# Block 0 of a Mish MLP by single x tiles, with one accumulation group per PSUM bank

## The chip, the cores and the metric

The kernel runs on one core of one Trainium2 chip. The metric is the device time of one execution in microseconds; lower is better. TensorE (PE in the profile, with PEld for its weight loads) multiplies; VectorE (DVE) and ScalarE (ACT) read the results out of PSUM; GpSimd (POOL) only prepares constants; SyncE (SP) and ACT issue the DMAs.

## The reference

```python
B, S, D, F = 1, 2048, 512, 1792        # bf16 inputs x, w1, b1, w2
def reference(x, w1, b1, w2):
    h = jnp.einsum("bsd,df->bsf", x, w1) + b1
    sp = jnp.log1p(jnp.exp(-jnp.abs(h))) + jnp.where(h > 0, h, jnp.zeros_like(h))
    act = h * jnp.tanh(sp)             # Mish
    return jnp.einsum("bsf,fd->bsd", act, w2)
```

Two matrix products with a Mish between them: x (2048 x 512) by w1 (512 x 1792) plus the bias, Mish, and then by w2 (1792 x 512).

## The kernel before

The 2048 rows of x are taken in four blocks of 512 (`NSB`, `SBW`). For each block the first product (mm1) makes h transposed, one f tile of 128 at a time: 14 f tiles (`FT`), each an accumulation over four k tiles (`KT`) of D, with w1 as the weights and x transposed (`xT`) as the moving operand of 512 columns. ScalarE applies Mish with the bias straight from PSUM into `a_sb` (L164). The second product (mm2) then makes four output tiles of 128 rows, each an accumulation over the 14 f tiles (L195); VectorE copies them to `o_sb` (L199) and SP stores them (L177). The order on every engine is the order in which the program is written: all mm1 of a block, its four mm2, the next block. There is no scheduler; each engine follows its own instruction list and waits on semaphores, which the small class `Stream` sets (`wait`, `mark`).

PSUM has eight banks in use. mm1 uses banks 4 to 7 in turn (`bank1`, L158), so an f tile has to wait for the Mish of the f tile four before it (L168). mm2 uses banks 0 to 3 in turn.

Blocks 1 to 3 get `xT` by transposing DMAs (L100). Block 0 is loaded as it is and transposed by PE: `half_T(h)` (L119) takes half h of the block, 256 rows, waits for its load, and for each k makes two transposes into one bank of 0 to 3; VectorE (even k, L132) and ScalarE (odd k, L135) copy them into `xT`. `first_mm1(h, ks)` (L137) multiplies the columns of one half, 256 of them, by the weights of f tiles 0 to 3 (`F0`) for the listed k tiles, into banks 4 to 7. Each half opens its own accumulation (`start=(k == 0)`), the second only once the first is complete.

The queues at the front: SP issues the two halves of x (256 KB each, a partition getting two neighbouring rows, so 2 KB in one piece, L86-87), then w1 of f tiles 4-7, w1 of f tiles 8-13, w2, and the three transposing loads. ACT issues w1 of f tiles 0-3 in two loads, k tiles 0-1 and 2-3 (L89-90), and the bias. PE starts with six dummy matmuls of 512 columns (L148), then `half_T(0)`, two dummies of 256 columns (`FILL`, L152), and the order of L204 to L215:

```python
        first_mm1(0, (0, 1))
        half_T(1)
        first_mm1(0, (2, 3))
        ...
        first_mm1(1, range(KT))
        for t in range(F0, FT):
            mm1(t)
```

Of the kernel before, what the change touches and what calls it, by code (L numbers as in the profile page):

```python
# [4 lines left out]

P = 128
N_WARM = 6
FILL = (256, 256)


class Stream:
# [20 lines left out]
def bass_standalone__dense_activation_mish__prompt_kernel(  # L32
# [8 lines left out]
    ACT = mybir.ActivationFunctionType  # L41
    ALU = mybir.AluOpType
    BF, F32 = dt.bfloat16, dt.float32

    _, S, D = x.shape
    F = w1.shape[1]
    KT, FT, SBW, C = D // P, F // P, 512, D - P
    NSB, JT = S // SBW, SBW // P
    assert (S, D, F) == (2048, 512, 1792)
    x2, out2 = x[0], out[0]  # L50
    w1v = w1.rearrange("(k p) f -> p k f", p=P)
    w2v = w2.rearrange("(j p) d -> p j d", p=P)
    F0 = 4

    with ExitStack() as es:
        def sb(name, shape, t):
            return es.enter_context(nc.sbuf_tensor(name, shape, t))

        x_nat = sb("x_nat", [P, JT, D], BF)
        xT = sb("xT", [P, KT, S], BF)  # L60
        w1_sb = sb("w1_sb", [P, KT, F], BF)
        w2_sb = sb("w2_sb", [P, FT, D], BF)
        b1_nat = sb("b1_nat", [FT, P], BF)
        b1_sb = sb("b1_sb", [P, FT], F32)
        ones = sb("ones", [P, P], BF)
        ident = sb("ident", [P, P], BF)
        a_sb = sb("a_sb", [P, NSB * FT, SBW], BF)
        o_sb = sb("o_sb", [P, NSB * JT, D], BF)
        ps = es.enter_context(nc.psum_tensor("ps", [P, 8, 512], F32))

        def sem(name):
            return es.enter_context(nc.semaphore(name))

        sp = Stream(nc.sync, None)
        pe = Stream(nc.tensor, sem("c_pe"))
        dve = Stream(nc.vector, sem("c_dve"))
        act = Stream(nc.scalar, sem("c_act"))
        pool = Stream(nc.gpsimd, sem("c_pool"))

        def load(q, dst, src, name, transpose=False):  # L80
            s = sem(name)
            (q.eng.dma_start_transpose if transpose else q.eng.dma_start)(dst, src).then_inc(s, 16)
            return (s, 16)


        x0v = x2[0:SBW, :].rearrange("(h p j) d -> p h j d", h=2, j=2)  # L86
        t_xn = [load(sp, x_nat[:, 2 * h:2 * h + 2, :], x0v[:, h], "s_xn%d" % h) for h in range(2)]
        t_w1k = []
        for k in (0, 2):  # L89
            t_w1k += [load(act, w1_sb[:, k:k + 2, 0:F0 * P], w1v[:, k:k + 2, 0:F0 * P], "s_w1k%d" % k)] * 2  # L90
        t_b1 = load(act, b1_nat[:, :], b1.rearrange("(j p) -> j p", p=P), "s_b1")
        t_w1 = {}
        for a, b in ((4, 8), (8, FT)):
            t = load(sp, w1_sb[:, :, a * P:b * P], w1v[:, :, a * P:b * P], "s_w1_%d" % a)
            for f in range(a, b):
                t_w1[f] = t
        t_w2 = load(sp, w2_sb[:, :, :], w2v, "s_w2")
        t_xT = [None]
        for s in range(1, NSB):
            t_xT.append(load(sp, xT[:, :, s * SBW:(s + 1) * SBW], x2[s * SBW:(s + 1) * SBW, :], "s_xT%d" % s, True))  # L100


        t_ones = pool.mark(pool.eng.memset(ones[:, :], 1.0))  # L103
        pool.wait(t_ones)
        t_id = pool.mark(pool.eng.affine_select(ident[:, :], ones[:, :], pattern=[[1, P]], compare_op=ALU.is_equal,  # L105
                                                fill=0.0, base=0, channel_multiplier=-1))
        act.eng.preload_act_table(ACT.Mish)  # L107


        c_w = nc.const_aps.tensor(1.0, [P, P], BF)  # L110
        c_m = nc.const_aps.tensor(1.0, [P, 512], BF)

        def dummy(n=512):
            nc.tensor.matmul(ps[:, 7, 0:n], c_w, c_m[:, 0:n], start=True, stop=True)  # L114

        HB = SBW // 2
        t_cp = [[None] * KT for _ in range(2)]

        def half_T(h):  # L119

            pe.wait(t_xn[h])
            for k in range(KT):
                if h == 1:
                    pe.wait(t_cp[0][k])
                psb = ps[:, k, 0:HB // 2].bitcast(BF)
                for j in range(2):
                    mm = nc.tensor.transpose(psb[:, j * P:(j + 1) * P], x_nat[:, 2 * h + j, k * P:(k + 1) * P], ident[:, :])  # L127
                t = pe.mark(mm)
                dst = xT[:, k, h * HB:(h + 1) * HB]
                if k % 2 == 0:  # L130
                    dve.wait(t)
                    t_cp[h][k] = dve.mark(nc.vector.tensor_copy(dst, psb))  # L132
                else:
                    act.wait(t)
                    t_cp[h][k] = act.mark(act.eng.activation(dst, psb, ACT.Copy))  # L135

        def first_mm1(h, ks):  # L137

            cs = slice(h * HB, (h + 1) * HB)
            for k in ks:  # L140
                for f in range(F0):
                    pe.wait(t_w1k[k], t_cp[h][k])
                    mm = nc.tensor.matmul(ps[:, 4 + f, cs], w1_sb[:, k, f * P:(f + 1) * P], xT[:, k, cs],  # L143
                                          start=(k == 0), stop=(k == KT - 1))
                    if h == 1 and k == KT - 1:
                        mish(f, pe.mark(mm))

        for _ in range(N_WARM):  # L148
            dummy()
        pe.wait(t_id)  # L150
        half_T(0)
        for n in FILL:  # L152
            dummy(n)


        t_mish = {}

        def bank1(t):  # L158
            return 4 + t % 4

        def mish(t, t_mm):
            act.wait(t_b1c, t_mm)
            f = t % FT
            t_mish[t] = act.mark(act.eng.activation(a_sb[:, t, :], ps[:, bank1(t), :], ACT.Mish, bias=b1_sb[:, f:f + 1]))  # L164

        def mm1(t):
            s, f = divmod(t, FT)
            pe.wait(t_mish.get(t - 4), t_w1.get(f), t_xT[s])  # L168
            for k in range(KT):
                mm = nc.tensor.matmul(ps[:, bank1(t), :], w1_sb[:, k, f * P:(f + 1) * P],  # L170
                                      xT[:, k, s * SBW:(s + 1) * SBW], start=(k == 0), stop=(k == KT - 1))
            mish(t, pe.mark(mm))

        def store(q, i, lo, hi, tok):
            q.wait(tok)
            rows = out2[i * P:(i + 1) * P, :] if i >= JT else o0v[:, i // 2, i % 2, :]
            q.eng.dma_start(rows[:, lo:hi], o_sb[:, i, lo:hi]).then_inc(s_out, 16)  # L177

        s_out = sem("s_out")
        o0v = out2[0:SBW, :].rearrange("(h p j) d -> p h j d", h=2, j=2)  # L180
        n_out = 0
        t_ev = {}

        def mm2(i):
            nonlocal n_out
            s, j = divmod(i, JT)
            pe.wait(t_w2)
            last = i == NSB * JT - 1
            parts = [(0, C, i % 4), (C, D, (i + 1) % 4)] if last else [(0, D, i % 4)]
            for lo, hi, bank in parts:  # L190
                pe.wait(*([t_ev[bank]] if bank in t_ev else [t_b1c, t_cp[1][1], t_cp[1][3]]))
                for f in range(FT):
                    t = s * FT + f
                    pe.wait(t_mish[t])
                    mm = nc.tensor.matmul(ps[:, bank, 0:hi - lo], a_sb[:, t, j * P:(j + 1) * P], w2_sb[:, f, lo:hi],  # L195
                                          start=(f == 0), stop=(f == FT - 1))
                t_mm = pe.mark(mm)
                dve.wait(t_mm)
                t_ev[bank] = dve.mark(nc.vector.tensor_copy(o_sb[:, i, lo:hi], ps[:, bank, 0:hi - lo]))  # L199
                store(sp, i, lo, hi, t_ev[bank])  # L200
                n_out += 1


        first_mm1(0, (0, 1))  # L204
        half_T(1)
        first_mm1(0, (2, 3))
        pe.wait(t_b1)
        psb1 = ps[:, 0, 256:256 + FT // 2].bitcast(BF)
        pe.wait(t_cp[1][0])
        t_b1t = pe.mark(nc.tensor.transpose(psb1, b1_nat[:, :], ident[0:FT, 0:FT]))  # L210
        dve.wait(t_b1t)
        t_b1c = dve.mark(nc.vector.tensor_copy(b1_sb[:, :], psb1))  # L212
        first_mm1(1, range(KT))
        for t in range(F0, FT):
            mm1(t)  # L215
        for s in range(NSB):
            for j in range(JT):
                mm2(s * JT + j)
            if s + 1 < NSB:
                for f in range(FT):  # L220
                    mm1((s + 1) * FT + f)
        sp.eng.wait_ge(s_out, 16 * n_out)


# [26 lines left out]
```

## Time and profile before

| | |
|---|---|
| median of 3 runs | 106.61 us (105.97 to 107.19) |
| the profiled execution | 107.43 us, of which the span from the first to the last instruction is 106.2 us |
| PE busy | 102.3 us, 96% of the span |
| ACT, DVE busy | 40.6 us (38%), 12.5 us (12%) |
| moved by DMA | 7.94 MB in 12417 packets |

How to read the rows: a row of the timeline has the start and the time of a run of like instructions, the engine (SPq and ACTq are the DMA-issuing queues), the line of the kernel, what is written and read, and in brackets how long the engine had been idle and what ended that. A row of the chain has the start, the time, and the work that the end of the program hung on then. A row of the windows has for each stretch its length, the busy time of each engine with its instructions, TensorE's granted clock, the mean busy share of the DMA engines, and GB/s. The clock column reads 1.00 throughout, also where matmuls follow each other at half rate, so the rate has to be read from the matmuls' starts. Matmul durations overlap: the time of one is its start to its modelled end.

### The profile page before, as it was taken

The numbers are of one execution on the slowest core, as the hardware profiler recorded it, in microseconds if no ns is written. First come the engines' busy times: TensorE is split into PE (matmuls) and PEld (weight loads), VectorE is DVE, ScalarE is ACT, GpSimd is POOL, SyncE is SP. The second block draws the span as 40 slices with busy tenths as digits, with TensorE's granted clock in tenths as the row PEclk, the third lists the DMA queues.
The fourth block names the chain that finished last, engine by engine and source line by source line (L and its number), as shares of the span: only waits on it lengthen the run. The fifth ranks groups of instructions, "written<-read, shape, count | busy, mean of one in ns | idle before, by whom it ended". The sixth has DMA issues, their size and how long they took to land.

```text
span 106.2 us, 1146 instructions
## 1 busy us (share of the span) xinstructions
PE 102.3 (96%) x503; PEld 48.7 (46%) x503; DVE 12.5 (12%) x22; ACT 40.6 (38%) x61; POOL 0.7 (1%) x6
## 2 busy tenths in 40 slices
PE   6798999999999999999999999999999999999992
PEld 2486444444444444444444444444444444444462
DVE  0210000022112000021122000021122000011223
ACT  0631988500005888600005777700004888700000
POOL 2000000000000000000000000000000000000000
DMA  2999999911111000001111000001111000001111
GB/s 60 330 374 357 348 286 244 141 40 49 49 49 49 0 0 6 0 0 49 49 49 49 0 0 3 0 6 49 49 49 49 0 0 0 0 0 54 51 49 49
DMA packets 12417, 7.94 MB, mean 75 GB/s; under 512 B 6780, under 2 KB 12156, under 8 KB 12412
## 3 DMA queue, kind: packets, MB, share of 16 engines
q1 hardware_dynamic: 11840, 7.34, 25.1%
q10 hardware_dynamic: 572, 0.53, 1.6%
q8 instruction: 4, 0.07, 0.3%
q14 instruction: 1, 0.01, 0.0%
HBM read 4.20 MB, written 2.10 MB: 59 GB/s over the span
## 4 chain that ended last, share of the span: by engine, by line
PE 94%; DMA 3%; ACT 1%; DVE 0%; issue 0%
PE ps L195 46%; PE ps L170 42%; PE ps L143 4%; DMA x_nat<-in_x_dram 3%; PE ps L127 1%; ACT a_sb L164 1%; PE ps L114 0%; DVE o_sb L199 0%; PE ps L210 0%
## 5 line engine op out<-in xcount | busy, mean ns | idle before, releaser
L164 ACT ACTIVATE a_sb<-ps,b_sb 128x512 bf16<-128x512 f32 x56 | 37.9, 688 | 47.0 <-PE ps L170 44.9
L195 PE MATMUL ps<-w_sb,a_sb 128*128 128x512 bf16 (+2 forms) x238 | 49.0, 366 | 0.0
L170 PE MATMUL ps<-xT,w_sb 128*128 128x512 bf16 x208 | 45.6, 379 | 0.5 <-ACT a_sb L164 0.5
L195 PEld LDWEIGHTS ps<-w_sb,a_sb 128*128 128x128 bf16 x238 | 22.8, 98 | 25.9
L170 PEld LDWEIGHTS ps<-xT,w_sb 128*128 128x128 bf16 x208 | 20.3, 98 | 25.1 <-ACT a_sb L164 0.8
L199 DVE CAST o_sb<-ps 128x512 bf16<-128x512 f32 (+2 forms) x17 | 11.2, 660 | 84.7 <-PE ps L195 84.7
L143 PE MATMUL ps<-xT,w_sb 128*128 128x256 bf16 x32 | 4.6, 297 | 0.0
L114 PE MATMUL ps<-const-bfloat16-1.0 128*128 128x512 bf16 (+1 forms) x8 | 3.3, 572 | 0.8 <-PEq L236 0.8
L143 PEld LDWEIGHTS ps<-xT,w_sb 128*128 128x128 bf16 x32 | 3.4, 109 | 0.7
L135 ACT ACTIVATE xT<-ps 128x256 bf16<-128x256 bf16 x4 | 1.4, 382 | 2.7 <-PE ps L127 2.7
L107 ACT ACT_TABLE_LOAD x1 | 1.3, 1283 | 2.5 <-issue 2.5
L127 PE MATMUL ps<-ident,x_nat 128*128 128x128 bf16 x16 | 1.6, 262 | 0.6 <-DMA x_nat<-in_x_dram 0.6
L127 PEld LDWEIGHTS ps<-ident,x_nat 128*128 128x128 bf16 x16 | 1.3, 117 | 1.5 <-issue 1.5
L132 DVE COPY xT<-ps 128x256 bf16<-128x256 bf16 x4 | 1.1, 292 | 6.6 <-PE ps L127 6.5
L114 PEld LDWEIGHTS ps<-const-bfloat16-1.0 128*128 128x128 bf16 x8 | 1.0, 137 | 1.9 <-issue 1.9
L105 POOL TENSOR_SCALAR_AFFINE_SELECT ident<-ones 128x128 bf16<-128x128 bf16 x1 | 0.3, 294 | 0.1
L212 DVE CAST b_sb<-ps 128x14 f32<-128x14 bf16 x1 | 0.2, 173 | 0.8 <-PE ps L210 0.8
L103 POOL MEMSET ones<- 128x128 bf16 x1 | 0.2, 205 | 0.3 <-POOLq L236 0.3
L210 PEld LDWEIGHTS ps<-ident,b_nat 14*128 14x128 bf16 x1 | 0.1, 90 | 0.2 <-issue 0.2
L210 PE MATMUL ps<-ident,b_nat 14*128 14x14 bf16 x1 | 0.2, 177 | 0.0
L236 POOL MEMSET const-bfloat16-1.0<- 128x1 bf16 x1 | 0.1, 103 | 0.0
L236 POOL MEMSET const-uint8-127<- 128x1 uint8 x1 | 0.1, 103 | 0.0
(2 smaller groups left out, 0.2 us busy)
## 6 DMA issues: line engine op xcount, KB each, us to landing
out_dram<-o_sb SPq DMA_DIRECT2D x15, 128.0 KB, 1.7
w_sb<-in_w_dram SPq DMA_DIRECT2D x1, 1792.0 KB, 12.2
w_sb<-in_w_dram SPq DMA_DIRECT2D x1, 768.0 KB, 7.6
w_sb<-in_w_dram ACTq DMA_DIRECT2D x2, 256.0 KB, 4.4
x_nat<-in_x_dram SPq DMA_DIRECT2D x2, 256.0 KB, 3.7
w_sb<-in_w_dram SPq DMA_DIRECT2D x1, 512.0 KB, 5.9
out_dram<-o_sb SPq DMA_DIRECT2D x1, 96.0 KB, 1.6
xT<-in_x_dram SPq DMA_TRANSPOSE x3, 5.7
```

What stands on the lines that cost most here:

```text
L105: t_id = pool.mark(pool.eng.affine_select(ident[:, :], ones[:, :], pattern=[[1, P]], compare_op=ALU.is_equal, fill=0.0, base=0, channel_mu ...
L107: act.eng.preload_act_table(ACT.Mish)
L114: nc.tensor.matmul(ps[:, 7, 0:n], c_w, c_m[:, 0:n], start=True, stop=True)
L127: mm = nc.tensor.transpose(psb[:, j * P:(j + 1) * P], x_nat[:, 2 * h + j, k * P:(k + 1) * P], ident[:, :])
L132: t_cp[h][k] = dve.mark(nc.vector.tensor_copy(dst, psb))
L135: t_cp[h][k] = act.mark(act.eng.activation(dst, psb, ACT.Copy))
L143: mm = nc.tensor.matmul(ps[:, 4 + f, cs], w1_sb[:, k, f * P:(f + 1) * P], xT[:, k, cs], start=(k == 0), stop=(k == KT - 1))
L164: t_mish[t] = act.mark(act.eng.activation(a_sb[:, t, :], ps[:, bank1(t), :], ACT.Mish, bias=b1_sb[:, f:f + 1]))
L170: mm = nc.tensor.matmul(ps[:, bank1(t), :], w1_sb[:, k, f * P:(f + 1) * P], xT[:, k, s * SBW:(s + 1) * SBW], start=(k == 0), stop=(k == KT ...
L195: mm = nc.tensor.matmul(ps[:, bank, 0:hi - lo], a_sb[:, t, j * P:(j + 1) * P], w2_sb[:, f, lo:hi], start=(f == 0), stop=(f == FT - 1))
L199: t_ev[bank] = dve.mark(nc.vector.tensor_copy(o_sb[:, i, lo:hi], ps[:, bank, 0:hi - lo]))
L210: t_b1t = pe.mark(nc.tensor.transpose(psb1, b1_nat[:, :], ident[0:FT, 0:FT]))
```

## The change

Block 0's x is loaded as tile 0, tile 1 (128 rows, 128 KB each) and tiles 2-3 (256 KB), a partition getting one row of 1 KB per tile. Each tile is transposed by itself: two k tiles into one bank, copied by VectorE (k 0-1) and ScalarE (k 2-3) into two column blocks of `xT`. Tiles 0 and 1 use banks 0 to 3, and tiles 2 and 3 the same again.

The matmuls of f tiles 0 to 3 run in the order in which tiles and weights come: tile 0 with k 0-1 (128 columns), tile 1 with k 0-1 (128 columns), tiles 0-1 with k 2 (256 columns), then the transposes of tiles 2 and 3, tiles 0-1 with k 3, tiles 2-3 with k 0-1, the bias, tiles 2-3 with k 2-3. Only the very first matmul into a bank carries the accumulation start. The two dummies of 256 columns are gone; the six of 512 stay. f tiles 4 to 7 of block 0 go into banks 0 to 3, which the transposes have used, and the others into banks 4 to 7 as before. The bias is copied into a zeroed 128 x 128 tile and transposed as 128 rows. `a_sb` is indexed by f tile and row instead of by block and f tile. The w1 and w2 loads keep their sizes; from f tile 4 on and for the blocks 1 to 3 the order of the matmuls is the same.

```diff
-        x0v = x2[0:SBW, :].rearrange("(h p j) d -> p h j d", h=2, j=2)
-        t_xn = [load(sp, x_nat[:, 2 * h:2 * h + 2, :], x0v[:, h], "s_xn%d" % h) for h in range(2)]
+        for j in range(2):
+            t_xn[j] = load(sp, x_nat[:, j, :], x2[j * P:(j + 1) * P, :], "s_xn%d" % j)
+        t_xn[2] = t_xn[3] = load(sp, x_nat[:, 2:4, :], x2[2 * P:4 * P, :].rearrange("(j p) d -> p j d", p=P), "s_xn2")
...
+        t_bz = dve.mark(nc.vector.memset(b1_pad[:, :], 0.0))
...
+        def transpose_x(j):
+            pe.wait(t_xn[j], t_id)
+            for h, eng in ((0, dve), (1, act)):
+                bank = 2 * (j % 2) + h
+                pe.wait(*free[bank])
+                psb = ps[:, bank, 0:P].bitcast(BF)
+                for i in range(2):
+                    k = 2 * h + i
+                    mm = nc.tensor.transpose(psb[:, i * P:(i + 1) * P], x_nat[:, j, k * P:(k + 1) * P], ident[:, :])
+                eng.wait(pe.mark(mm))
+                dst = xT[:, 2 * h:2 * h + 2, j * P:(j + 1) * P]
+                src = psb.rearrange("p (k t) -> p k t", k=2)
+                t = eng.mark(nc.vector.tensor_copy(dst, src) if eng is dve else act.eng.activation(dst, src, ACT.Copy))
+                t_cp[j, h] = t
+                free[bank] = [t]
...
+        def mm1_step(s, f, k, bank, js=None):
+            n = BLOCKS[s]
+            lo, hi = (0, n) if js is None else (js[0] * P, (js[-1] + 1) * P)
+            first = k == 0 and lo == 0
+            if first:
+                pe.wait(*free[bank])
+            pe.wait(t_w1[k, f])
+            if s:
+                pe.wait(t_xT[s])
+            else:
+                pe.wait(*[t_cp[j, k // 2] for j in (js or range(N0))])
+            return nc.tensor.matmul(ps[:, bank, lo:hi], w1_sb[:, k, f * P:(f + 1) * P],
+                                    xT[:, k, starts[s] + lo:starts[s] + hi], start=first, stop=(k == KT - 1 and hi == n))
...
+        for n in WARM:
+            dummy(n)
+        transpose_x(0)
+        transpose_x(1)
+        def first(js, ks):
             for k in ks:
                 for f in range(F0):
+                    mm = mm1_step(0, f, k, 4 + f, js)
+                    if k == KT - 1 and js[-1] == N0 - 1:
+                        mish(0, f, 4 + f, pe.mark(mm))
+        first((0,), (0, 1))
+        first((1,), (0, 1))
+        first((0, 1), (2,))
+        transpose_x(2)
+        transpose_x(3)
+        dve.wait(t_b1, t_bz)
+        t_b1p = dve.mark(nc.vector.tensor_copy(b1_pad[0:FT, :], b1_nat[:, :]))
+        first((0, 1), (3,))
+        first((2, 3), (0, 1))
+        pe.wait(t_b1p, *free[0])
+        psb1 = ps[:, 0, 0:P // 2].bitcast(BF)
+        t_b1t = pe.mark(nc.tensor.transpose(psb1, b1_pad[:, :], ident[:, :]))
         dve.wait(t_b1t)
+        t_b1c = dve.mark(nc.vector.tensor_copy(b1_sb[:, :], psb1[:, 0:FT]))
+        free[0] = [t_b1c]
+        first((2, 3), (2, 3))
+        for f in range(F0, FT):
+            mm1(0, f, {4: 0, 5: 1, 6: 2, 7: 3}.get(f, 4 + f % 4))
+        for i in range(N0):
+            mm2(i, 0, D, i)
```

More of the change, by code (lines that the diff above doesn't have):

```diff
@@ L6 @@
 P = 128
-N_WARM = 6
-FILL = (256, 256)
+WARM = (512,) * 6
+BLOCKS = (512, 512, 512, 512)
 class Stream:
@@ L46, in bass_standalone__dense_activation_mish__prompt_kernel @@
     F = w1.shape[1]
-    KT, FT, SBW, C = D // P, F // P, 512, D - P
-    NSB, JT = S // SBW, SBW // P
-    assert (S, D, F) == (2048, 512, 1792)
+    KT, FT = D // P, F // P
+    assert (S, D, F) == (2048, 512, 1792) and sum(BLOCKS) == S
     x2, out2 = x[0], out[0]
@@ L52, in bass_standalone__dense_activation_mish__prompt_kernel @@
     w2v = w2.rearrange("(j p) d -> p j d", p=P)
+    starts = [sum(BLOCKS[:i]) for i in range(len(BLOCKS) + 1)]
     F0 = 4
+    N0 = BLOCKS[0] // P
     with ExitStack() as es:
@@ L57, in sb @@
             return es.enter_context(nc.sbuf_tensor(name, shape, t))
-        x_nat = sb("x_nat", [P, JT, D], BF)
+        x_nat = sb("x_nat", [P, N0, D], BF)
         xT = sb("xT", [P, KT, S], BF)
@@ L63, in bass_standalone__dense_activation_mish__prompt_kernel @@
         b1_nat = sb("b1_nat", [FT, P], BF)
+        b1_pad = sb("b1_pad", [P, P], BF)
         b1_sb = sb("b1_sb", [P, FT], F32)
@@ L66, in bass_standalone__dense_activation_mish__prompt_kernel @@
         ident = sb("ident", [P, P], BF)
-        a_sb = sb("a_sb", [P, NSB * FT, SBW], BF)
-        o_sb = sb("o_sb", [P, NSB * JT, D], BF)
+        a_sb = sb("a_sb", [P, FT, S], BF)
+        o_sb = sb("o_sb", [P, S // P, D], BF)
         ps = es.enter_context(nc.psum_tensor("ps", [P, 8, 512], F32))
@@ L83, in load, with load_w1 @@
             return (s, 16)
-        x0v = x2[0:SBW, :].rearrange("(h p j) d -> p h j d", h=2, j=2)
-        t_xn = [load(sp, x_nat[:, 2 * h:2 * h + 2, :], x0v[:, h], "s_xn%d" % h) for h in range(2)]
-        t_w1k = []
-        for k in (0, 2):
-            t_w1k += [load(act, w1_sb[:, k:k + 2, 0:F0 * P], w1v[:, k:k + 2, 0:F0 * P], "s_w1k%d" % k)] * 2
+        def load_w1(q, ks, a, b):
+            return load(q, w1_sb[:, ks, a * P:b * P], w1v[:, ks, a * P:b * P], "s_w1_%d_%d" % (ks.start, a))
+        t_xn, t_w1, t_w2 = [None] * N0, {}, {}
+        for ks in (slice(0, 2), slice(2, 4)):
+            t = load_w1(act, ks, 0, F0)
+            for f in range(F0):
+                for k in range(ks.start, ks.stop):
+                    t_w1[k, f] = t
+        for j in range(2):
+            t_xn[j] = load(sp, x_nat[:, j, :], x2[j * P:(j + 1) * P, :], "s_xn%d" % j)
+        t_xn[2] = t_xn[3] = load(sp, x_nat[:, 2:4, :], x2[2 * P:4 * P, :].rearrange("(j p) d -> p j d", p=P), "s_xn2")
         t_b1 = load(act, b1_nat[:, :], b1.rearrange("(j p) -> j p", p=P), "s_b1")
-        t_w1 = {}
         for a, b in ((4, 8), (8, FT)):
-            t = load(sp, w1_sb[:, :, a * P:b * P], w1v[:, :, a * P:b * P], "s_w1_%d" % a)
+            t = load_w1(sp, slice(0, KT), a, b)
             for f in range(a, b):
-                t_w1[f] = t
-        t_w2 = load(sp, w2_sb[:, :, :], w2v, "s_w2")
+                for k in range(KT):
+                    t_w1[k, f] = t
+        t = load(sp, w2_sb[:, :, :], w2v, "s_w2")
+        for f in range(FT):
+            t_w2[f] = t
         t_xT = [None]
-        for s in range(1, NSB):
-            t_xT.append(load(sp, xT[:, :, s * SBW:(s + 1) * SBW], x2[s * SBW:(s + 1) * SBW, :], "s_xT%d" % s, True))
+        for s in range(1, len(BLOCKS)):
+            lo, hi = starts[s], starts[s + 1]
+            t_xT.append(load(sp, xT[:, :, lo:hi], x2[lo:hi, :], "s_xT%d" % s, True))
+        t_bz = dve.mark(nc.vector.memset(b1_pad[:, :], 0.0))
         t_ones = pool.mark(pool.eng.memset(ones[:, :], 1.0))
@@ L111, in bass_standalone__dense_activation_mish__prompt_kernel, with dummy @@
         c_m = nc.const_aps.tensor(1.0, [P, 512], BF)
-        def dummy(n=512):
+        def dummy(n):
             nc.tensor.matmul(ps[:, 7, 0:n], c_w, c_m[:, 0:n], start=True, stop=True)
[L116 to L121, printed above, removed]
-            for k in range(KT):
[L123 to L135, printed above, removed]
@@ L137, in first_mm1 @@
-        def first_mm1(h, ks):
-            cs = slice(h * HB, (h + 1) * HB)
+        free = [[] for _ in range(8)]
+        t_cp = {}
+        t_mish = {}
+        def transpose_x(j):
[13 more added lines that the diff above has]
+                free[bank] = [t]
@@ new lines, in mish @@
+        def mish(s, f, bank, t_mm):
+            n = BLOCKS[s]
+            act.wait(t_b1c, t_mm)
+            t = act.mark(act.eng.activation(a_sb[:, f, starts[s]:starts[s + 1]], ps[:, bank, 0:n], ACT.Mish,
+                                            bias=b1_sb[:, f:f + 1]))
+            t_mish[s, f] = t
+            free[bank] = [t]
+        def mm1_step(s, f, k, bank, js=None):
+            n = BLOCKS[s]
+            lo, hi = (0, n) if js is None else (js[0] * P, (js[-1] + 1) * P)
[9 more added lines that the diff above has]
+                                    xT[:, k, starts[s] + lo:starts[s] + hi], start=first, stop=(k == KT - 1 and hi == n))
@@ new lines, in mm1, with mm2_step @@
+        def mm1(s, f, bank):
+            for k in range(KT):
+                mm = mm1_step(s, f, k, bank)
+            mish(s, f, bank, pe.mark(mm))
+        s_out = sem("s_out")
+        n_out = 0
+        def mm2_step(i, f, lo, hi, bank):
+            s = max(b for b in range(len(BLOCKS)) if starts[b] <= i * P)
+            if f == 0:
+                pe.wait(*free[bank])
+            pe.wait(t_w2[f], t_mish[s, f])
+            return nc.tensor.matmul(ps[:, bank, 0:hi - lo], a_sb[:, f, i * P:(i + 1) * P], w2_sb[:, f, lo:hi],
+                                    start=(f == 0), stop=(f == FT - 1))
@@ new lines, in put, with mm2 @@
+        def put(i, lo, hi, bank, t_mm):
+            nonlocal n_out
+            dve.wait(t_mm)
+            t = dve.mark(nc.vector.tensor_copy(o_sb[:, i, lo:hi], ps[:, bank, 0:hi - lo]))
+            free[bank] = [t]
+            sp.wait(t)
+            sp.eng.dma_start(out2[i * P:(i + 1) * P, lo:hi], o_sb[:, i, lo:hi]).then_inc(s_out, 16)
+            n_out += 1
+        def mm2(i, lo, hi, bank):
+            for f in range(FT):
+                mm = mm2_step(i, f, lo, hi, bank)
+            put(i, lo, hi, bank, pe.mark(mm))
@@ L140, in first_mm1 @@
+        for n in WARM:
[3 more added lines that the diff above has]
+        def first(js, ks):
             for k in ks:
                 for f in range(F0):
[L142 to L201, printed above, removed]
@@ L204, in bass_standalone__dense_activation_mish__prompt_kernel @@
[L204 to L210, printed above, removed]
-        dve.wait(t_b1t)
[L212 to L221, printed above, removed]
+                    mm = mm1_step(0, f, k, 4 + f, js)
@@ new lines, in bass_standalone__dense_activation_mish__prompt_kernel @@
+        t_b1t = pe.mark(nc.tensor.transpose(psb1, b1_pad[:, :], ident[:, :]))
+        dve.wait(t_b1t)
+        t_b1c = dve.mark(nc.vector.tensor_copy(b1_sb[:, :], psb1[:, 0:FT]))
[5 more added lines that the diff above has]
+            mm2(i, 0, D, i)
+        for s in range(1, len(BLOCKS)):
+            for f in range(FT):
+                mm1(s, f, 4 + f % 4)
+            for i in range(starts[s] // P, starts[s + 1] // P):
+                if i < S // P - 1:
+                    mm2(i, 0, D, i % 4)
+                else:
+                    mm2(i, 0, D - P, i % 4)
+                    mm2(i, D - P, D, (i + 1) % 4)
```

## The prediction

> **What bounds the kernel now.** I read the page first, for the busy shares, then the chain of work that ended last, for where TensorE (PE) is not streaming.
>
> ```profile
> span 106.2 us, 1146 instructions
> PE 102.3 (96%) x503; PEld 48.7 (46%) x503; DVE 12.5 (12%) x22; ACT 40.6 (38%) x61; POOL 0.7 (1%) x6
> ...
> 0.81 3.25 DMA x_nat<-in_x_dram
> ...
> 4.20 1.01 PE ps L127 x8
> 5.21 0.43 PE ps L114 x2
> 5.63 1.41 PE ps L143 x8
> 7.04 0.45 PE ps L127 x8
> 7.49 0.87 PE ps L143 x8
> 8.36 0.11 PE ps L210
> 8.47 1.65 PE ps L143 x14
> 10.12 0.68 ACT a_sb L164
> ...
> 10.84 8.81 PE ps L170 x40
> 19.65 12.09 PE ps L195 x56
> ...
> 92.17 12.13 PE ps L195 x70
> ...
> 104.33 0.29 DVE o_sb L199
> ```
>
> From 10.84 us to 104.3 us the chain is PE alone: 56 matmuls of 512 columns take 12.09 us, 0.216 us each, without a gap. The change leaves the order and number of these matmuls alone (40, then 56 seven times in turn), so what it can move is the instant at which f tile 4 begins, 10.84 us here. I call it E. What follows E lasts 106.2 - 10.84 = 95.4 us.
>
> Before E the timeline shows PE's rate and the two places where it stands still.
>
> ```profile
> 0.84 2.72 PE L114 MATMUL ps<-const-bfloat16-1.0 128*128 128x512 bf16 x6 [0.84 <-PEq L236]
> ...
> 4.20 1.01 PE L127 MATMUL ps<-ident,x_nat 128*128 128x128 bf16 x8 [0.64 <-DMA x_nat<-in_x_dram]
> ...
> 5.43 1.61 PE L143 MATMUL ps<-xT,w_sb 128*128 128x256 bf16 x8
> ...
> 6.88 0.61 PE L127 MATMUL ps<-ident,x_nat 128*128 128x128 bf16 x8
> 7.19 0.51 DVE L132 COPY xT<-ps 128x256 bf16<-128x256 bf16 x2 [1.87 <-PE ps L127]
> ...
> 8.40 1.92 PE L143 MATMUL ps<-xT,w_sb 128*128 128x256 bf16 x16
> ...
> 10.10 4.23 ACT L164 ACTIVATE a_sb<-ps,b_sb 128x512 bf16<-128x512 f32 x7 [2.14 <-PE ps L143]
> ...
> 10.84 8.81 PE L170 MATMUL ps<-xT,w_sb 128*128 128x512 bf16 x40 [0.52 <-ACT a_sb L164]
> ```
>
> PE waits 0.64 us for the first half of x and 0.52 us for the first Mish, which frees bank 4. And it has two rates. The six dummies of 512 columns take 2.72 us, 0.45 each against 0.216 later: about half speed. Eight matmuls of 256 columns run from 5.43 to 6.88, 1.45 us, where eight at full rate take 0.87 (7.49). With 0.213 us slow and 0.108 fast, 5.6 of the eight were slow, so the rate doubled near 5.43 + 5.6 x 0.213 = 6.6 us. I use 0.107 slow and 0.056 fast for 128 columns (0.45 us for eight transposes at 7.04).
>
> The transfers in front of all this:
>
> ```profile
> 0.80 0.98 ACTq L82 DMA_DIRECT2D w_sb<-in_w_dram  x2
> 0.81 0.87 SPq L82 DMA_DIRECT2D x_nat<-in_x_dram  x2
> ...
> w_sb<-in_w_dram ACTq DMA_DIRECT2D x1, 256.0 KB, 3.9
> ...
> x_nat<-in_x_dram SPq DMA_DIRECT2D x1, 256.0 KB, 4.2
> w_sb<-in_w_dram ACTq DMA_DIRECT2D x1, 256.0 KB, 4.9
> ...
> 1.00:2.53 1.53, 1.53 (x5) 0.47 (x4) 0.00 (x0) 0.00 (x0) 0.30 (x2) 1.00 0.45 84
> 2.53:3.03 0.50, 0.50 (x3) 0.12 (x1) 0.00 (x0) 0.48 (x1) 0.00 (x0) 1.00 0.87 270
> 3.03:3.56 0.53, 0.53 (x2) 0.00 (x0) 0.00 (x0) 0.53 (x1) 0.00 (x0) 1.00 0.93 226
> 3.56:3.96 0.40, 0.00 (x0) 0.00 (x0) 0.00 (x0) 0.27 (x1) 0.00 (x0) 1.00 0.96 328
> 3.96:4.66 0.70, 0.47 (x5) 0.49 (x6) 0.06 (x1) 0.00 (x0) 0.00 (x0) 1.00 1.06 386
> 4.66:5.35 0.69, 0.69 (x8) 0.62 (x6) 0.53 (x2) 0.49 (x2) 0.00 (x0) 1.00 1.07 380
> ```
>
> The first four rows are issues; the number after the KB is the time to landing. Each queue issues a load every 0.43 to 0.49 us, so the second x half starts at 1.25 us and the second w1 load at 1.29. The landings are: x half 0 at 4.06 (the chain), w1 for k 0-1 at 0.80 + 3.9 = 4.7, x half 1 at 5.45, w1 for k 2-3 at 6.2. The last column of the windows is GB/s; times the window's length it gives 129, 264, 384, 515, 785 and 1047 kB moved by the ends of the six rows. One load is 262 kB. If they are served one behind the other in order of issue, x half 0 is through at 3.03, w1 k 0-1 at 3.96, x half 1 at 4.66 and w1 k 2-3 at 5.35; each landed 1.03, 0.74, 0.79 and 0.85 us later. The same lag each time is what supports this order.
>
> **The change part by part.**
>
> *Arrivals.* x comes as 131, 131 and 262 kB on SP, alternating with the two w1 loads on ACT. By the running totals: x tile 0 through at 2.53, landed 3.3 to 3.6; w1 k 0-1 (393 kB) through just past 3.56, landed 4.3 to 4.6; x tile 1 (524 kB) in the place that w1 k 0-1 has now, landed 4.7; w1 k 2-3 (785 kB) 5.5; x tiles 2-3 6.2. For tile 1, which decides, the bounds are 3.8 (262 kB through at 3.03 and the smallest lag, if no w1 went ahead of it) and 5.45 (where x half 1 lands now). I take 4.7, the row with the same total. That a tile now comes in pieces of half the size (1 KB rows) has its row in the w1 loads, whose rows are 1 KB too.
>
> *Head of PE.* The dummies end at 3.56 as now. T0 (four transposes) starts at 3.56 and ends at 3.99; PE then waits 0.7 us for tile 1. T1: 4.7 to 5.13. Tile 0's eight matmuls (k 0-1, four f tiles, 128 columns): 8 x 0.107, to 5.98. Tile 1's eight: slow until 6.6 (5.8 of them), 2.2 fast, to 6.72. The two fillers (0.43 us in the chain) are gone; they covered the copies, and here that cover is T1 and the other tile's matmuls: VectorE's copy of two columns blocks, 0.26 us by its row and begun 0.31 us after its transposes, is done at about 5.4 for tile 1 where PE wants it at 5.98.
>
> *The rest of block 0 from 6.72, all at full rate:* k 2 of tiles 0-1, 4 x 0.108 = 0.43; eight transposes 0.45 (tiles 2-3 landed at 6.2, wanted at 7.15); k 3, 0.43; k 0-1 of tiles 2-3, 0.87; the bias transpose 0.11, as now though with 128 rows; k 2-3 of tiles 2-3, 0.87. Together 3.16, which puts E at 9.88. The copies of tiles 2-3 lie beside k 3: the second VectorE copy ends 0.31 + 2 x 0.26 = 0.83 us after the transposes start, PE wants it after 0.88. If that cover failed by a copy, it would cost 0.26.
>
> *f tiles 4 to 7 in banks 0 to 3.* Today the last sixteen matmuls start at 8.40 and would be over at 8.40 + 16 x 0.108 = 10.13; f tile 4 starts at 10.84, behind the first Mish. So the wait is worth 0.71 (0.52 by the idle column alone, which models matmul ends late). It goes. Next late would be bank 4 for f tile 8: it starts at E + 16 x 0.216 = 13.3, and the first Mish ends near 10.2. Banks 0 to 3 were emptied by the copies before the last sixteen matmuls.
>
> *Edits at nothing.* One accumulation start per bank instead of two, the new shape of a_sb, the padded bias (a small VectorE copy and a memset, both long before PE's bias transpose at 8.9; today PE takes the bias at 8.36 without a wait). SP issues one load more, so everything behind it on SP starts 0.43 later:
>
> ```profile
> w_sb<-in_w_dram SPq DMA_DIRECT2D x1, 1792.0 KB, 12.2
> w_sb<-in_w_dram SPq DMA_DIRECT2D x1, 768.0 KB, 7.6
> ...
> w_sb<-in_w_dram SPq DMA_DIRECT2D x1, 512.0 KB, 5.9
> ...
> 3.38 16.74 SPq L82 DMA_TRANSPOSE xT<-in_x_dram  x3
> ```
>
> Issued from 1.73 us on, the 512 KB of f tiles 4-7 land at 7.6, then 8.1 (wanted at 9.9); the 768 KB by 10.3 (wanted at 13.3); w2 by 15.4 (wanted at E + 40 x 0.216 = 18.5). The transposing loads leave SP at 20.1, then 20.5; the first store follows its matmuls by then.
>
> *Sum.* E goes from 10.84 to 9.88, so 0.96 us less: span 105.2, and the profiled execution's 107.43 would be 106.5. That execution is 0.8 us above the median of the three runs, and slow PE at the front is one thing in which it may differ from them. If PE ran fast from the first transpose, today's head would be 4.20 + 0.45 + 0.22 + 0.87 + 0.45 = 6.2, as w1 k 2-3 lands, then 0.87 + 0.11 + 2.44 (8.40 to 10.84) = 9.6; the new one 4.7 + 0.22 + 0.87 = 5.8, plus 3.16 = 8.95. That is 0.67. Between the two I take 0.9: 106.61 - 0.9 = **105.7 us**, 0.85% less. About 1% is what a measurement of this kernel can tell from no change, so the forecast is a gain that lies within that.
>
> **The rivals.**
>
> *The clock is late (slower).* PE worked slowly for 2.72 us before its gap of 0.64 and 2.4 after it, 5.1 in all, ahead of the doubling at 6.6. The new head has no fillers and a gap of 0.7 at 4.0 to 4.7. If a gap there starts the count anew and 5.1 us of unbroken work are needed, the doubling comes at 4.7 + 5.1 = 9.8: tile 1's matmuls end at 6.84, 2.98 us of slow work do 1.49 of the 3.16, and E is 9.8 + 1.67 = 11.5. That is 0.65 later than now: 107.3. It is slower than before once the doubling comes after 8.5 us (6.84 + 3.16 + half of what lies between 6.84 and it exceeds 10.84). For it: the slow first 2.72 us alone did not bring full rate. Against: the present gap of 0.64, almost as long, did not prevent it at 6.6, and if only the 2.4 us behind the gap count, the doubling comes at 7.1 and the gain is still 0.7. [...]
>
> *The queues share evenly.* If SP's and ACT's loads took turns packet by packet, w1 k 2-3 would end together with x tiles 2-3, at 1047 kB, and land at 6.2. Slow PE reaches it at 6.72 and loses nothing; fast PE would wait from 5.8 to 6.2: gain about 0.3 to 0.6, 106.1. Against it: x half 1, in 2 KB pieces, and w1 k 0-1, in 1 KB pieces, would now both land at 5.4; w1 k 0-1 landed at 4.7. [...]
>
> *Tile 1 lands late, and only the Mish wait goes.* At 5.45, T1 ends at 5.88, and tile 0's and tile 1's matmuls at 7.1; E is 10.25, a gain of 0.6: 106.0. For it: three small loads on SP, each with a lag of its own. That tile 0 be no earlier than half 0 is now (4.06) would by itself change nothing, as T0 would still end before tile 1 comes.
>
> *Tile 1 lands early.* At 3.8 to 4.2 the matmuls of tile 0 start by w1 k 0-1's 4.3 to 4.6, and E is about 9.6, a gain of 1.2: 105.4.
>
> **How the numbers follow.** Forecast 0.50 (105.7; 105.4 to 106.0), early tile 1 0.13 (105.4), late tile 1 0.15 (106.0), even sharing 0.05 (106.1), late clock 0.17 (107.3). The range runs from 104.9, the early case with the runs' scatter (0.6 below their median), to 107.3, the clock case. Faster by over 1% is below 105.54: most of the early case and a third of the forecast, 0.28. Slower by over 1% is above 107.7: the clock case reaches from 106.6 to 108.9 (slow through all of the head, E = 6.84 + 2 x 3.16 = 13.2), and I put 0.10 of its 0.17 above that line. The rest is 0.62.
>
> **What the profile would show.** Right: transposes from about 3.6 us, a wait of PE for x near 4.0 to 4.7, full rate from 6.6, no wait of the f tile 4 group for Mish, E near 9.9, and 95.4 us behind it. Wrong: a landing of x tile 1 away from 4.7 moves E by up to its own size; 256-column matmuls still 0.21 us apart after 7 us is the clock; a wait of PE for w1 at k 2 is the sharing; and a gap anywhere after E would be something I have not seen.

## The result

| | kernel before | changed kernel |
|---|---|---|
| median of 20 runs | 106.81 us (105.97 to 107.35) | 105.94 us (105.34 to 106.74) |
| profiled execution | 107.43 us, span 106.2 us | 105.42 us, span 104.2 us |

The ratio is 0.9922, 95% interval 0.9896 to 0.9948: 0.83 us less (0.56 to 1.11). In a later series it was 0.9927 (0.9899 to 0.9954). Executions about 2 us longer, which came in all three series of experiments and in whose four profiles PE's rate doubles only at 8.7 to 10.2 us, are left out of the ratios.

The two profiled executions lie 2.0 us apart, more than twice what the ratio gives. The chain of the changed kernel, start and time in us, then what:

```profile
span 104.2 us, 1154 instructions
PE 100.7 (97%) x500; PEld 48.1 (46%) x509; DVE 12.7 (12%) x24; ACT 40.3 (39%) x61; POOL 0.7 (1%) x6
...
1.27 2.93 DMA x_nat<-in_x_dram
...
4.25 0.51 PE ps L142 x4
4.76 1.33 PE ps L170 x20
6.09 0.02 issue
6.11 0.62 PE ps L142 x8
6.73 1.40 PE ps L170 x12
8.12 0.06 PE ps L226
8.18 0.87 PE ps L170 x8
...
9.11 8.58 PE ps L170 x39
17.69 2.16 PE ps L186 x10
...
102.36 0.29 DVE o_sb L192
```

No ACT stands ahead of f tile 4 any more. (The 39 and 10 stand for 40 and 56 with breaks: a few matmul records are missing from this trace.) Starts are read better from the timeline:

```profile
0.84 2.72 PE L126 MATMUL ps<-const-bfloat16-1.0 128*128 128x512 bf16 x6 [0.84 <-PEq L259]
...
3.35 0.63 PE L142 MATMUL ps<-ident,x_nat 128*128 128x128 bf16 x4
...
4.25 0.51 PE L142 MATMUL ps<-ident,x_nat 128*128 128x128 bf16 x4 [0.27 <-DMA x_nat<-in_x_dram]
...
4.59 1.49 PE L170 MATMUL ps<-xT,w_sb 128*128 128x128 bf16 x20
...
6.11 0.62 PE L142 MATMUL ps<-ident,x_nat 128*128 128x128 bf16 x8
...
6.56 1.56 PE L170 MATMUL ps<-xT,w_sb 128*128 128x256 bf16 x12
...
8.02 9.67 PE L170 MATMUL ps<-xT,w_sb 128*128 128x256 bf16 x47
...
8.83 6.13 ACT L153 ACTIVATE a_sb<-ps,b_sb 128x512 bf16<-128x512 f32 x10 [1.63 <-PE ps L170]
...
17.52 2.75 PE L186 MATMUL ps<-w_sb,a_sb 128*128 128x512 bf16 x11
```

The last eight matmuls of the first four f tiles start at 8.02, so f tile 4 starts at E = 8.02 + 8 x 0.108 = 8.9 us, and mm2 at 17.52. The kernel before, same view:

```profile
19.48 4.70 PE L195 MATMUL ps<-w_sb,a_sb 128*128 128x512 bf16 x21
```

mm2 starts 1.96 us earlier, which is nearly the whole difference of the spans: 104.2 - 8.9 = 95.3 us behind E, as before. But PE's rate doubled at a different moment. The 20 matmuls from 4.76, worth 24 of 128 columns, take 1.33 us, 0.055 each: full rate already. Tile 1's four transposes take 4.59 - 4.25 = 0.34 us, two slow and two fast, so the doubling is near 4.5 us, against 6.6 in the profile before. A pair of single profiles compares this moment as well as the kernels.

The transfers (queue, size, time from issue to landing; and three of the windows with GB/s last):

```profile
w_sb<-in_w_dram ACTq DMA_DIRECT2D x1, 256.0 KB, 3.1
x_nat<-in_x_dram SPq DMA_DIRECT2D x1, 128.0 KB, 2.4
...
w_sb<-in_w_dram ACTq DMA_DIRECT2D x1, 256.0 KB, 4.1
x_nat<-in_x_dram SPq DMA_DIRECT2D x1, 256.0 KB, 4.3
x_nat<-in_x_dram SPq DMA_DIRECT2D x1, 128.0 KB, 2.9
...
1.00:2.53 1.53, 1.53 (x5) 0.47 (x4) 0.00 (x0) 0.00 (x0) 0.30 (x2) 1.00 0.29 90
2.53:3.03 0.50, 0.50 (x3) 0.12 (x1) 0.00 (x0) 0.49 (x1) 0.00 (x0) 1.00 1.01 336
3.03:3.56 0.53, 0.53 (x4) 0.30 (x3) 0.00 (x0) 0.53 (x1) 0.00 (x0) 1.00 1.20 367
```

Tile 0 landed at 0.81 + 2.4 = 3.2, w1 k 0-1 at 3.9, tile 1 at 4.2, w1 k 2-3 at 1.29 + 4.1 = 5.4, tiles 2-3 at 1.73 + 4.3 = 6.0 (6.06 to two places). The order is the forecast one; the first three are 0.1 to 0.7 us earlier. By 3.56 us 500 kB had moved (138 + 168 + 194), where before it was 384.

### The profile page after: what moved, and what is told of

It is laid out like the page before. It is cut to its first block, busy times and chain, and to the rows that moved or that the text cites. A ratio compares the mean times of both kernels' runs of the same rounds, so it can differ in the third digit from the quotient of the medians.

```text
span 104.2 us, 1154 instructions
## 1 busy us (share of the span) xinstructions
PE 100.7 (97%) x500; PEld 48.1 (46%) x509; DVE 12.7 (12%) x24; ACT 40.3 (39%) x61; POOL 0.7 (1%) x6
## 4 chain that ended last, share of the span: by engine, by line
PE 94%; DMA 3%; issue 1%; SPq 0%; DVE 0%
PE ps L170 46%; PE ps L186 46%; DMA x_nat<-in_x_dram 3%; PE ps L142 1%; SPq L84 0%; DVE o_sb L192 0%; PE ps L226 0%
## 5 line engine op out<-in xcount | busy, mean ns | idle before, releaser
L170 PE MATMUL ps<-xT,w_sb 128*128 128x512 bf16 (+2 forms) x243 | 49.1, 358 | 0.3
L192 DVE CAST o_sb<-ps 128x512 bf16<-128x512 f32 (+2 forms) x17 | 11.2, 660 | 83.0 <-PE ps L186 83.0
L126 PE MATMUL ps<-const-bfloat16-1.0 128*128 128x512 bf16 x6 | 2.7, 623 | 0.8 <-PEq L259 0.8
```

The lines of the kernel that those rows point to most:

```text
L170: return nc.tensor.matmul(ps[:, bank, lo:hi], w1_sb[:, k, f * P:(f + 1) * P], xT[:, k, starts[s] + lo:starts[s] + hi], start=first, stop=( ...
L192: t = dve.mark(nc.vector.tensor_copy(o_sb[:, i, lo:hi], ps[:, bank, 0:hi - lo]))
```

## The experiments

My theory after the result: the gain is the Mish wait (about 0.7 us), the tile order adds little, and the moment at which PE's rate doubles makes the scatter of both kernels. The rivals: the gain comes from the arrivals and the tile order; from the dropped fillers; or the wait of PE for tiles 2-3 holds back more gain.

**The bank map, taken away and given alone.**

```diff
  (changed kernel)
-            mm1(0, f, {4: 0, 5: 1, 6: 2, 7: 3}.get(f, 4 + f % 4))
+            mm1(0, f, 4 + f % 4)
```

> The changed kernel with f tiles 4 to 7 of block 0 back in banks 4 to 7, so that f tile 4 waits for the first Mish again; all else is kept. My theory: the Mish wait is worth 0.55 to 0.7 us and nothing hides it, so this kernel comes out 0.6 us above the changed one, near 106.5 us, and PE shows a wait of about 0.5 us for ScalarE ahead of f tile 4. The rival, that the gain of 0.8 us is all from the arrivals and the order of block 0, expects no difference: 105.9 us.

> The changed kernel with f tiles 4 to 7 in banks 4 to 7, again, for a narrower interval (it was 0.994 to 1.0035). If the tile order by itself gains nothing, the ratio to the kernel before is within 0.998 to 1.001; if it gains the 0.25 us that my sum leaves it beside the 0.71 of the wait, 0.997 or less.

Measured: 0.9987 of the kernel before (0.9939 to 1.0035), and on another chip 0.9985 (0.9965 to 1.0005), 106.5 us at the median. Without the bank map the changed kernel, with all its other edits, is not distinguishable from the kernel before. Its chain and timeline, first profile:

```profile
9.36 0.70 ACT a_sb L153
10.06 0.05 issue
10.10 8.81 PE ps L170 x40
...
8.55 1.04 PE L170 MATMUL ps<-xT,w_sb 128*128 128x256 bf16 x8
10.10 2.12 PE L170 MATMUL ps<-xT,w_sb 128*128 128x512 bf16 x9 [0.52 <-ACT a_sb L153]
```

The wait is back, behind the first Mish of 0.70: the last eight matmuls would be over at 8.55 + 8 x 0.108 = 9.41, and f tile 4 starts at 10.10, 0.69 us later (0.52 by the idle column, as in the kernel before). The second profile agrees: 105.1 - 95.3 puts its E at 9.8, behind a Mish that ends at 9.8.

```diff
  (kernel before; f tiles 8-11 and mm2 wait for the banks' last users accordingly)
-            return 4 + t % 4
+            return t - 4 if 4 <= t < 8 else 4 + t % 4
```

> The kernel before with f tiles 4 to 7 of block 0 in banks 0 to 3 and nothing else changed. My theory expects the gain of the wait alone, 0.6 to 0.7 us: 106.15 us, a ratio of 0.994. The rival (arrivals and order make the gain) expects the time of before, 106.8 us.

> The kernel before with f tiles 4 to 7 of block 0 in banks 0 to 3, again, since most of its first executions doubled PE's rate late and left one time to compare. If the bank map alone makes the gain: a ratio of 0.993 to the kernel before, 105.9 to 106.1 us. If the order of block 0 is needed for it: 0.997 or more.

The first time one execution took 105.9 us, against 106.7, and the other five 107.9 to 108.5; the profiled one of these doubled its rate near 8.7 us. One time is too few for a ratio. The second gave 0.9941 (0.9915 to 0.9967), 0.63 us less. So by the point values one line of the bank map brings three quarters of what the whole change brings. Chain and timeline of the second profile show what becomes late there:

```profile
1.80 5.89 DMA b_nat<-in_b_dram
...
7.74 0.18 PE ps L214
7.92 1.85 PE ps L143 x16
...
6.55 1.04 PE L143 MATMUL ps<-xT,w_sb 128*128 128x256 bf16 x8
```

With the rate doubled early (its eight transposes of half 0, from 4.49 us, were already fast), PE is through with half 0 at 6.55 + 8 x 0.109 = 7.4, waits 0.3 us for the bias, landed at 7.7, and only then takes the last sixteen matmuls. The changed kernel wants the bias after tiles 2-3's k 0-1, at 8.0 us even at full rate.

**The fillers.**

```diff
  (kernel before with the new bank map)
-FILL = (256, 256)
+FILL = ()
```

> The same with the two dummies of 256 columns left out. They take 0.43 us of PE at the slow rate and 0.22 at the fast one; my theory puts them on the path whenever PE and not a load is late, so 0.2 to 0.3 us less: 105.9 us, which would leave nothing of the median gain for the tile order itself. A rival: the fillers keep PE at work and bring the doubling of its rate forward; then leaving them out gains nothing or costs up to 0.5 us: 106.2 to 106.7.

> The same without the two dummies of 256 columns, again. On the path they are worth 0.2 to 0.4 us (ratio 0.990 to 0.991); hidden behind the load of w1 for k 2-3 or given back by a later doubling of the rate, nothing or less (0.993 or more).

Again the first run left one time (105.85 us), too few for a reading. The second: 0.9951 (0.9929 to 0.9972), against 0.9941 with the fillers. No gain from leaving them out can be told; the 0.990 to 0.991 expected if they were on the path is outside the interval. The chain says why:

```profile
4.60 0.30 DVE xT L132
4.91 1.88 PE ps L143 x8
```

Without them PE stands until VectorE's copy is over at 4.9 us; the fillers filled that wait. Whether they also bring the doubling of the rate forward, these runs do not tell.

**A filler in the changed kernel.**

```diff
         transpose_x(0)
+        dummy(256)
         transpose_x(1)
```

> The changed kernel with one dummy of 256 columns between the transposes of tile 0 and those of tile 1, where PE waited 0.27 us for the load. The late clock theory (the scatter of the changed kernel, 105.34 to 106.74, is wider than the loads and a doubling by 6.6 us allow, so in its slow executions the rate doubles later than that, because of its gaps) expects the upper end of the times to fall by about 0.4 us and the median by 0.1 to 0.2. The rival, that the moment of doubling is not touched by so small a gap, expects the same median within 0.1 us and the same scatter.

> The changed kernel with one dummy of 256 columns between the transposes of tiles 0 and 1, again. The gap theory expects no execution above 106.8 us (the changed kernel had one of twelve at 107.4) and a ratio of 0.992; the rival, that the gap does not matter, expects one execution in ten near 107.4 or above and the same ratio.

Measured 0.9948 (0.9898 to 0.9998) and, on another chip, 0.991 (0.988 to 0.9939). None of the twelve executions was above 106.5 us, where the changed kernel had one of twelve at 107.4 in its later series and none above 106.74 in its first twenty. That agrees with the gap theory (that PE's wait for tile 1 delays the doubling) but is too few to show it, the two were not run in one series, and the changed kernel's 0.9922 and 0.9927 lie between the two ratios. In the first of these profiles the last tiles came late:

```profile
7.15 0.62 PE L142 MATMUL ps<-ident,x_nat 128*128 128x128 bf16 x8 [0.90 <-DMA x_nat<-in_x_dram]
```

PE stood 0.90 us for tiles 2-3, landed at 7.1; with its last eight matmuls starting at 9.06, E was 9.9, although the rate had doubled by 4.8. So a late landing of these tiles moves E as well, and the doubling is not all of the scatter.

With the second of these runs one chip has four versions side by side, if the dummy is taken as worth nothing: the kernel before, 1; with the new bank map alone, 0.9941; with all the rest but the old map, 0.9985; with both, 0.991 (0.988 to 0.9939). There the map is worth 0.63 us in the old order and 0.80 in the new, and the order 0.16 us with the old map and 0.33 with the new. The intervals for the order overlap in both pairs, those for the map in neither.

**The changed kernel again, and what delays tiles 2-3.** After the repeat, two edits, one for the shape of the load and one for its neighbour in the queues:

```diff
-x2[2 * P:4 * P, :].rearrange("(j p) d -> p j d", p=P)
+x2[2 * P:4 * P, :].rearrange("(p j) d -> p j d", j=2)      # stores of output tiles 2, 3 likewise
...
-        t_b1 = load(act, b1_nat[:, :], ...)
+        t_b1 = load(pool, b1_nat[:, :], ...)               # behind the identity on GpSimd
```

> The changed kernel as it is, beside the kernel before on this chip. Earlier on one chip the kernel before took 106.7 us, the same with f tiles 4 to 7 in banks 0 to 3 took 105.9, and the changed kernel with f tiles 4 to 7 in banks 4 to 7 took 106.6. If the wait explains the gain, the changed kernel takes 105.9 here. Its profile shows a wait for x tiles 2-3, between 0 and 0.9 us, as the three profiles with this front have had it (tiles landed at 6.06, 6.59 and 7.10 us); the theory that this landing sets the start of f tile 4 in these executions expects that start 3.0 us after the landing.

> The changed kernel with tiles 2-3 of x loaded as pairs of neighbouring rows (2 KB pieces, as the kernel before loads x) and their output rows put back accordingly. In the profiles the last engine's share of this load landed 0.5 to 1.5 us after the median share. If the 1 KB pieces of it cause the late share, the load lands by 5.7 us, PE waits less than 0.1 us for it, and the time falls by 0.2 to 0.5 us. If its place in the order, behind everything else, is the cause, it lands at 6.0 to 7.1 as now and the time stays within 0.1 us.

> The changed kernel with the bias (14 pieces of 256 bytes) loaded by GpSimd's queue instead of ScalarE's, where it stands beside x tiles 2-3 in the order of issue. If the bias disturbs the load of tiles 2-3, that load lands by 5.7 us, with the last engine's share within 0.4 us of the median, and the time falls by 0.2 to 0.5 us; if not, landing and time stay.

The repeat gave 0.9927 (0.9899 to 0.9954), 105.69 us; in its profile the tiles landed at 6.2, just as PE came for them, and E was 9.06. In the two profiles in which PE did wait, E followed the landing by 2.8 us (6.06 to 8.89, 7.1 to 9.93). Row pairs: landed at 5.8, between the two expectations, ratio 0.9944 (0.9908 to 0.998). Bias by GpSimd: landed at 6.3, ratio 0.9931 (0.99 to 0.9962). Neither brings anything, so neither the 1 KB pieces nor the bias is shown to be the cause of the landings from 5.8 to 7.1 us; with one profile of each, that stays open. The row pairs' profile fell on a late doubling and so shows its price:

```profile
5.32 2.56 PE ps L170 x20
7.88 0.85 PE ps L142 x8
8.73 1.64 PE ps L170 x12
10.37 0.06 PE ps L227
10.43 0.87 PE ps L170 x8
```

The 20 matmuls take 2.56 us, 0.107 per 128 columns, and the transposes 0.106 each: slow. The next twelve take 1.64 where slow would be 2.56 and fast 1.30, so the doubling came near 9.3 us. The span is 106.4, so E is 106.4 - 95.3 = 11.1.

**No dummies.**

```diff
-WARM = (512,) * 6
+WARM = ()
```

> The changed kernel without its six dummy matmuls. The late clock theory needs work of PE ahead of the doubling of its rate: with the first work at 3.3 us instead of 0.84, the doubling comes at 8 us or later in every execution, k 2 starts near 6.4 us at the slow rate, and f tile 4 starts 0.6 to 1.7 us later than now: 106.6 to 107.6 us, nearly all of the gain or more than it. The rival, that the rate doubles at a moment which does not depend on the work, expects the time unchanged within 0.2 us.

Measured 1.0066 of the kernel before (1.0033 to 1.01), 107.38 us. Against the 0.9927 of the changed kernel in the same series that is 1.4%, 1.5 us, for work on data that nobody reads. Its profile, which is that of the fastest of the twelve executions (106.46 us):

```profile
4.92 2.37 PE L170 MATMUL ps<-xT,w_sb 128*128 128x128 bf16 x20
...
7.13 0.61 PE L142 MATMUL ps<-ident,x_nat 128*128 128x128 bf16 x8
...
9.03 3.19 PE L170 MATMUL ps<-xT,w_sb 128*128 128x256 bf16 x17
```

From 4.92 to 7.13 us there is work of 24 times 128 columns; at 2.2 us about 17 of the 24 were slow, so the rate doubled at about 6.8, not at 8 us or later as I expected of every execution, and E was 9.03 + 0.87 = 9.9. That the slower eleven doubled later is likely but not shown.

## Why the prediction was right

*The time.* 105.7 us was forecast, 105.94 measured; 0.85% less forecast, 0.78% measured. Most of the 0.24 us is the kernel before, whose median is 106.81 over twenty runs and was 106.61 over the three that I had.

*The Mish wait* (0.71, between 0.52 and 0.71): right, and the main term. The bank map alone gives 0.63 us (0.35 to 0.91), and taking it out of the changed kernel puts 0.69 us of PE's waiting back.

*What the tile order adds* (0.96 - 0.71 = 0.25 in my sum, 0.67 - 0.71 = -0.04 in the one for full rate from the start): of the right smallness. The changed kernel with the old bank map is 0.16 us below the kernel before, with an interval from 0.37 less to 0.05 more, so it may be nothing. Part of my 0.25 were the fillers, 0.43 us of PE in the chain of the kernel before; alone they are worth nothing that can be told, since they lay over a copy.

*The landing of tile 1* (4.7): 4.20, 4.54, 4.34, 4.68, 4.66, 4.83, 4.48, 4.36 and 4.38 in the nine profiles of the changed front, a mean of 4.5. The order of issue held and the even sharing did not: w1 k 2-3 landed at 5.4 in the changed kernel's profile, ahead of tiles 2-3 at 6.06, and the pieces moved there show the two queues served mostly by whole loads in turn (up to 2.6 us 133 pieces from SP and 35 from ACT, from 2.6 to 3.1 us 15 and 162, from 3.1 to 3.6 us 108 and 86, from 3.6 to 4.5 us 71 and 245, from 4.5 to 5.2 us 223 and 40). My rival let the queues alternate piece by piece; only the stretch from 3.1 to 3.6 us, near one to one, looks like that.

*E.* The forecast of 9.88 was for a doubling at 6.6 us. The changed kernel's own profile had 8.9 with a doubling at 4.5 (my sum for full rate from the start: 8.95). The one profile of this front with a doubling near 6.6 to 6.8 is that without dummies: 9.9. At the medians, an estimate with 1.26 us outside the span and 95.3 behind E, the kernel before has E at 10.25 and the changed one at 9.4. Both lie between my two sums (9.6 and 10.84; 8.95 and 9.88), and I had both about half a microsecond late, which cancels in the difference. That the gain lay between 0.67 and 0.96 followed from the sums; that 0.9 came so close was a choice between them and in part luck.

*The late clock.* I gave it 0.17 and a time of 107.3, by E = 10 us plus half of what the doubling lies behind 6.84 us. It did not come in the twenty runs, but it exists: one execution of twelve in the later series took 107.42, and the profile with the doubling at 9.3 has E at 11.1, where that sum says 11.2. But it does not belong to the new head, as my rival had it: in one series the kernel before took 108.4 to 109.3 us in eight of eleven executions, and the two profiles of its head taken there, with the new bank map and one without the fillers, double at 8.7 and 10.2. What sets the moment was not settled. The doublings read from the profiles lie between 4.5 us or earlier and 10.2 us for fronts that differ little.

*What I had not listed:* PE's wait for tiles 2-3 (up to 0.90 us), where I had them land 0.9 us before PE wanted them. At full rate there was no such margin: in the changed kernel's profile they landed at 6.06 and PE took them at 6.11. The kernel before has its counterpart, the bias, which in its own profile PE took at 8.29 without a wait, and for which it stood 0.3 us in the second profile with the new bank map alone.

## What to carry to other kernels

When a chain shows PE waiting for the evacuation of one bank at a change of phase, look for banks whose last users are long done before reordering anything: here that single map is worth 0.6 to 0.8 us, most of the gain. Filler work and waits can cover each other at the front of a kernel, as here 0.43 us of fillers lay over a copy (0.9941 with them, 0.9951 without); price each against what is behind it, not by its own length. Where two single profiles differ by more than the repeated times do, here 2.0 against 0.83 us, read the moment at which PE's rate doubles in each before putting the difference down to the change.

## What the runs showed of the hardware that I had not expected

The moment of the doubling scatters from 4.5 us or earlier to 10.2 us after the start of the program, with the same six dummies from 0.84 us on. TensorE's granted clock reads 1.000 in all of these profiles. How much of the scatter of 1.4 us within each kernel the doubling makes is not shown, since tiles 2-3 landing at 7.1 instead of 6.06 us moved E by 1.0 us too. The changed kernel's profile moved more early on, with the first bytes in both profiles at about 1.8 us: 500 kB by 3.56 us, against 384 in the kernel before; whether the size of the pieces, that of the loads or neither makes it is not shown. And a bias of 3.5 KB, issued at 1.80 us behind half a megabyte of weights, needed 5.9 us to land in the second profile with the new bank map alone.
